# A fused attention, gating and channel-mix kernel on one core: another list of order for the opening and for the attention's pairs, and eleven pieces of the opening on another engine or queue

## The chip, the cores and the metric

The kernel runs as one program on one core of a Trainium2 chip. Its five engines are TensorE (PE), VectorE (DVE), ScalarE (ACT), GpSimd (POOL) and SyncE (SP, which only issues transfers here); each runs its own list of instructions in order and waits on semaphores for the others. The metric is the time of one execution on the device in microseconds (us). Three runs of the kernel before took 661.72, 662.39 and 663.0 us; the median is 662.39. The profile comes from one execution of its own.

## What is computed

Inputs are float32; batch 4, 8 heads, 576 positions, head size 64. Only the attention lies in the part that is changed:

```python
scores = scale * np.matmul(q, k.transpose(0, 1, 3, 2))
causal = np.triu(np.ones((S, S), dtype=bool), k=1)
cum = np.cumsum(np.maximum(s, 0.0), axis=-1)
bias = -(cum[:, :, :, None] - cum[:, :, None, :])
scores = np.where(causal, -1e9, scores + np.minimum(bias, 0.0))
scores = scores - np.max(scores, axis=-1, keepdims=True)
attn = np.exp(scores)
attn = attn / (np.sum(attn, axis=-1, keepdims=True) + 1e-09)
x = np.matmul(attn, v)
```

What follows is a gated layer (relu of x @ w_in, normalisation, a mixing over positions with w_spatial, w_out) and a channel mix (shifted x, w_k, a square, w_v, a sigmoid gate by w_r).

## The kernel before, in words

The 32 heads are worked in 16 pairs (two heads of one batch). A pair p passes through four stages that different engines share:

- T(p), function `st_T`: q and k, loaded as float32 into `RAW`, are split into a rounded high part and a low rest. `wh` and `xh` copy the high parts of q and k, `ud` and `vd` copy these to a second place, `ul` and `vl` subtract to get the rests. They are written into one large tile, `big`, which holds three pairs. In the opening each runs per head (a digit 0 or 1 behind the name).
- S(p), `st_S`: twelve score matmuls `s0` to `s11` (L459; 64 to 448 columns, six a head). VectorE takes the row maximum of each with the mask (L465, tile `jk`, accumulated in `mx`). `Ma` and `Mb` turn a head's maxima by a transpose on TensorE (L477), copy them on ACT (L479, tile `mt`) and send them as a row into `big` (L480).
- E(p), `st_E`: scores again with the maxima and the running sums as extra rows of the contraction (L497, two matmuls each, `e0` to `e9`, and `ez`, L530), the exponential on ACT (L517, L534), the causal mask on GpSimd (L521, L535).
- V(p), `st_V`: values (L555, L556, L559; `a0` to `a4` for one head, `b0` to `b4` for the other), copied out by ACT (L570, `fa`, `fb`). The sums of the exponentials go through memory (`n1`, `n2`, `n2b`), and `n30` on VectorE and `n31` on GpSimd multiply by their reciprocal (L592).

Beside these run small steps that decode weights from float64, part by part: `dL` loads (L125), `dF` is on ACT (L133, L134), `dD` on VectorE and GpSimd (L139 to L147), `dT` splits, `dS` stores (L182).

Before the first scores the running sums of s must be there: `lds` loads s, `sums` (L378, L379) sums them, `bases` (L103 by VectorE, L109 by GpSimd) takes the value at the start of each block of 128, `sums2` (L387, a copy, L389) splits the rest. `rx00` and `rx01` (L396) send the rows for pair 0 into `big`, `augd` (L403) keeps those of all pairs in memory. Constants `cw0` to `cw2` and `cx0` to `cx2` fill the rows of `big` that stay the same.

The order is written by hand in strings of these names. `START` has the opening: T, S and E of pair 0, T and S of pair 1, T of pair 2, and, with a plus, the whole of step 1 (E(1), V(0), S(2), T(3)). `ORDER` is the list for the steps 2 to 12: step p holds E(p), V(p-1), S(p+1) and T(p+2). `ORDER13` and `ORDER14` are for the steps 13 and 14. Each engine's own list follows from the strings, from `ENGINE` (V VectorE, S ACT, P GpSimd, by key; the letters A, B, C ahead of a key are the pairs 0, 1, 2 of the opening) and from `QUEUE` (A: issued by ACT; anything else: by SP). ACT issues a transfer in its own list, between its other instructions.

Of the kernel before, what the change touches and what calls it, by code (L numbers as in the profile page):

```python
# [26 lines left out]
def tile_kernel(  # L27
# [665 lines left out]
    START = """mask pads0 cx0 dD dT cw0 tiny ldk01 lds ldk00 cx1 dL ldq1 ldq01 pads2 sums 0xh0 ltv0 0xh1 1wh1 dF
               cx2 ldq00 0wh1 0vd1 bases sums2 0vd0 0ul1 0wh0 dL rx00 cw1 ldk1 rx01 0ul0 s0 ldq2 augd 1rows 1xh1 s4
               s10 s11 s9 s1 0vl0 s3 lv1 s2 cw2 1wh0 s5 0ud1 s6 s8 Ma pads1 0ud0 2wh1 dL s7 1xh0 2ul1 dF 1ul0 lv0
               1vd1 Mb e0 1vd0 0vl1 1s0 1s4 ldk2 1s6 dD 1vl0 dL e1 1s2 ez 2wh0 1ul1 e5 1s11 2rows 2xh1 dS 1s3 2vd1
               2ud1 1ud0 1s8 1s1 +lv 1s5 e3 2xh0 1s7 ldq3 1Ma 2vd0 1s9 +s6 1ud1 1s10 e4 e9 +s5 ones 2vl1 e6 e8 e7
               2ul0 dF +s4 +s9 1Mb e2 dT 2vl0 +ldk ldq4 1vl1 +e0 +zero +wh +s3 +a0 +s2 +s0 dL +a3 +ul ldk3 +e1 2ud0
               +xh +e3 +a1 +e5 +s1 +a2 dF +a4 +fa +ud +s10 +e4 +ez +s8 +e7 +rows +Ma +s7 +b0 +b3 +b2 +s11 +b1 dS
               +Mb +b4 +fb +e2 +n1 +e9 +e8 +e6 +ldq dD"""  # L700
# [744 lines left out]
```

## Time and profile before

| | before |
|---|---|
| runs (median of 3) | 662.39 us |
| the profiled execution: its time | 659.89 us |
| its span, first to last instruction | 658.1 us |
| TensorE busy | 628.7 us (96%) |
| VectorE busy | 519.8 us (79%) |
| ACT busy | 418.4 us (64%) |
| GpSimd busy | 337.3 us (51%) |
| granted TensorE clock, mean | 0.999 |

Busy shares are means over stages with different limits; a stretch has to be read by itself. Matmuls are pipelined and their ends are modelled, so a busy TensorE isn't TensorE at its peak. The time of the execution lies 1.8 us above its span, and 2.5 us below the median of the runs.

### The profile page before, as it was taken

The numbers are of one execution on the slowest core, as the hardware profiler recorded it, in microseconds if no ns is written. First come the engines' busy times: TensorE is split into PE (matmuls) and PEld (weight loads), VectorE is DVE, ScalarE is ACT, GpSimd is POOL, SyncE is SP. The second block draws the span as 40 slices with busy tenths as digits, with TensorE's granted clock in tenths as the row PEclk, the third lists the DMA queues.
The fourth block names the chain that finished last, engine by engine and source line by source line (L and its number), as shares of the span: only waits on it lengthen the run. The fifth ranks groups of instructions, "written<-read, shape, count | busy, mean of one in ns | idle before, by whom it ended". The sixth has DMA issues, their size and how long they took to land.

```text
span 658.1 us, 12257 instructions
## 1 busy us (share of the span) xinstructions
PE 628.7 (96%) x4036; PEld 551.9 (84%) x4036; DVE 519.8 (79%) x1168; ACT 418.4 (64%) x942; POOL 337.3 (51%) x464
## 2 busy tenths in 40 slices
PE   2899999999998999999999999999999999999997
PEld 1576666766666889999999999999999999999996
DVE  9879999999973799998878984888675866777773
ACT  5688888888874465575565572657675855554441
POOL 6357877759697434768646874531221123322220
PEclk9999999999999999999999999999999999999999
DMA  6446566565539727866454597743337973333301
GB/s 153 114 112 173 140 153 155 144 165 148 140 94 287 208 97 213 235 205 202 139 192 138 174 340 249 290 150 100 118 120 234 370 252 120 119 99 97 97 33 65
DMA packets 92303, 109.12 MB, mean 166 GB/s; under 512 B 32443, under 2 KB 73563, under 8 KB 90448
## 3 DMA queue, kind: packets, MB, share of 16 engines
q1 hardware_dynamic: 91146, 107.06, 53.7%
q10 hardware_dynamic: 1094, 1.28, 0.8%
q8 instruction: 32, 0.52, 0.3%
q14 instruction: 31, 0.25, 0.1%
HBM read 69.77 MB, written 37.52 MB: 163 GB/s over the span
## 4 chain that ended last, share of the span: by engine, by line
PE 71%; DVE 13%; DMA 7%; issue 3%; ACT 3%; POOL 1%; SPq 1%; DVEq 0%; POOLq 0%; ACTq 0%
PE mm L1009 26%; PE mm L757 24%; PE mm L825 7%; DVE big L121 4%; PE ps L497 4%; DVE jk L465 3%; PE pv L559 3%; PE s L459 3%; DMA rd<-r 2%; PE pv L556 1%; DMA rb<-rd 1%; DMA r<-pt 1%; ACT pt L570 1%; DMA brow<-in_moe_w_spatial_dram 1%; DVE g L139 1%
## 5 line engine op out<-in xcount | busy, mean ns | idle before, releaser
L757 PE MATMUL mm<-big 128*128 128x288 f32 (+1 forms) x600 | 102.6, 330 | 0.0
L757 PEld LDWEIGHTS mm<-big 128*128 128x128 f32 x600 | 91.5, 188 | 8.6 <-issue 0.4
L497 PE MATMUL ps<-big 128*128 128x288 f32 (+3 forms) x320 | 88.3, 369 | 1.7 <-ACT e L517 1.5
L147 POOL TENSOR_TENSOR f<-f,raw 128x256 int32<-128x256 int32 x64 | 52.3, 818 | 48.5 <-DVE f L145 19.9
L517 ACT ACTIVATE e<-ps 128x288 f32<-128x288 f32 (+3 forms) x160 | 62.5, 418 | 14.4 <-PE ps L497 12.4
L497 PEld LDWEIGHTS ps<-big 128*128 128x128 f32 x320 | 56.1, 199 | 17.5 <-issue 7.1
L465 DVE CUSTOM_DVE_ANT_0 jk<-s,mask 128x320 bf16<-128x320 f32 (+4 forms) x160 | 62.6, 423 | 9.8 <-PE s L459 7.9
L459 PE MATMUL s<-big 128*128 128x288 f32 (+4 forms) x192 | 54.8, 351 | 15.5 <-DMA big<-big 11.6
L559 PE MATMUL pv<-e,vp 128*65 128x448 f32 (+2 forms) x192 | 64.1, 434 | 0.0
L825 PE MATMUL mm<-xs,vb 128*128 128x288 f32 x256 | 56.3, 295 | 0.8 <-DVE vb L121 0.8
L521 POOL TENSOR_SCALAR_AFFINE_SELECT e<-e 128x128 f32<-128x128 f32 x128 | 46.8, 388 | 17.6 <-ACT e L517 15.3
L459 PEld LDWEIGHTS s<-big 128*128 128x128 f32 x192 | 35.7, 206 | 22.8 <-issue 13.5
L757 PE MATMUL mm<-wo,gh 128*128 128x512 f32 x216 | 52.4, 391 | 0.0
L757 PE MATMUL mm<-gh,wo 128*128 128x288 f32 x256 | 51.7, 294 | 0.0
L981 POOL TENSOR_TENSOR gh<-hl,gh 128x512 fp32r<-128x512 f32 x9 | 15.6, 1737 | 67.7 <-ACT gh L1215 67.7
L1009 PE MATMUL mm<-big,vb 128*128 128x256 f32 x384 | 48.4, 279 | 0.5 <-ACT vf L1158 0.5
L1009 PEld LDWEIGHTS mm<-big,vb 128*128 128x128 f32 x384 | 47.1, 188 | 1.3 <-ACT vf L1158 0.7
L121 DVE TENSOR_TENSOR big<-qk,big 64x1152 fp32r<-64x1152 f32 (+1 forms) x37 | 46.6, 1265 | 2.1 <-ACT big L106 0.9
L757 PEld LDWEIGHTS mm<-wo,gh 128*128 128x128 f32 x216 | 39.3, 188 | 7.5
L825 PEld LDWEIGHTS mm<-xs,vb 128*128 128x128 f32 x256 | 42.7, 188 | 1.2 <-DVE vb L121 1.2
L757 PEld LDWEIGHTS mm<-gh,wo 128*128 128x128 f32 x256 | 41.2, 188 | 0.2
L559 PEld LDWEIGHTS pv<-e,vp 128*65 128x65 f32 x192 | 25.1, 137 | 18.3 <-issue 14.1
(178 smaller groups left out, 1622.3 us busy)
## 6 DMA issues: line engine op xcount, KB each, us to landing
qk<-in_qk_dram SPq DMA_DIRECT2D x28, 288.0 KB
vf<-kd SPq DMA_DIRECT2D x6, 1024.0 KB
kd<-rt SPq DMA_DIRECT2D x32, 144.0 KB
rb<-rd SPq DMA_DIRECT2D x15, 288.0 KB
raw<-in_moe_w_in_dram SPq DMA_DIRECT2D x16, 256.0 KB
vp<-in_v_dram SPq DMA_DIRECT2D x16, 256.0 KB
raw<-in_moe_w_k_dram SPq DMA_DIRECT2D x16, 256.0 KB
raw<-in_moe_w_v_dram SPq DMA_DIRECT2D x16, 256.0 KB
```

Of the source, the lines that this page charges most:

```text
L121: (nc.gpsimd if eng == "P" else nc.vector).tensor_tensor(op=ALU.subtract, **kw)
L147: nc.gpsimd.tensor_tensor(out=f, in0=f, in1=low, op=ALU.add)
L459: nc.tensor.matmul(out=ps[:, 0:kn], lhsT=W[g][:, h, 128 * i:128 * i + 128], rhs=X[g][:, x0:x0 + kn], start=True, stop=True,)
L465: nc.vector.tensor_tensor_reduce(out=jk[r0:128, 0:kn], in0=ps[r0:128, 0:kn], in1=mask[r0:128, m0:m0 + kn], scale=1.0, scalar=(dst if mid e ...
L497: nc.tensor.matmul(out=ps[:, o:o + b - a], lhsT=st[g][:, key0(h, 128 * j):key0(h, 128 * j) + 128], rhs=mv[g][:, h, 64 + a:64 + b], start=( ...
L517: nc.scalar.activation(out=e[:, o:o + n], in_=ps[:, 0:n], func=ACTF.Exp, scale=scale)
L521: nc.gpsimd.affine_select(out=d, in_=d, pattern=[[1, w]], base=0, channel_multiplier=-1, compare_op=ALU.is_ge, fill=0.0,)
L559: nc.tensor.matmul(out=pv[0:VW, 1, 448 - w:448], lhsT=lt, rhs=e[:, OFF[j]:OFF[j] + w] if j < 4 else es[p][:, w * h:w * h + w], start=False ...
L757: nc.tensor.matmul(out=ps, lhsT=x, rhs=y, start=(m == 0), stop=(m == n - 1))
L825: nc.tensor.matmul(out=o, lhsT=x[:, sc, dd], rhs=y[:, sc, t], start=(sc == 0 and m == 0), stop=False)
L981: (nc.gpsimd if ENGINE[key] == "P" else nc.vector).tensor_tensor(**kw)
L1009: nc.tensor.matmul(out=ps, lhsT=x, rhs=y, start=(m == 0 and nm in ("P1", "P2", "P5")), stop=(m == last_m), skip_group_check=True)
```

## The change

Nothing that is computed changes. Two strings of order are rewritten, `ORDER` (steps 2 to 12) and `START`; `ORDER13`, `ORDER14` and all behind them stay. In `ENGINE` five keys of the opening move: two fills go to ACT (`cx0` from VectorE, `cx2` from GpSimd), `bases` goes from VectorE to GpSimd, pair 0's `xh` of the second head from ACT to GpSimd and its `ud` from VectorE to ACT. In `QUEUE` six transfers move: the loads of k for pair 0's second head, of q for pair 1 and of k for pair 3 from ACT to SP, and pair 0's q of the second head and its two rows of maxima from SP to ACT.

```diff
     ENGINE = dict(
...
-        cx0="V", cx2="P", bs="V", Axh1="S", Aud1="V",
+        cx0="S", cx2="S", bs="P", Axh1="P", Aud1="S",
...
     QUEUE = dict(
...
-        ldq1="A", Ma="P", Mb="P", ldq01="P", ldk01="A", ldk3="A",
+        ldq1="P", Ma="A", Mb="A", ldq01="A", ldk01="P", ldk3="P",
...
-    ORDER = """s4 s0 wh dT s6 e0 s3 e1 ul a0 vd e4 dL n2 s8 a3 lv xh e5 ltv zero s11 s5 rows a1 n2b e3 a2 a4 fa e2
-               dD e6 s2 dS ud s1 s7 b0 vl b3 Ma ldk s10 n31 e9 dF s9 e7 b1 b2 Mb b4 fb n1 n30 e8 ez ldq"""
+    ORDER = """s0 dT s4 wh s6 e0 s3 e1 e4 a0 ul dL vd n2 s8 a3 lv ltv xh s5 e5 zero s11 e3 a2 a1 a4 fa rows dD ud
+               e6 s2 n2b e2 s7 dS s1 vl b0 s10 b3 Ma s9 ldk dF n31 e9 e7 b1 b2 Mb b4 fb n1 ldq n30 e8 ez"""
...
-    START = """mask pads0 cx0 dD dT cw0 tiny ldk01 lds ldk00 cx1 dL ldq1 ldq01 pads2 sums 0xh0 ltv0 0xh1 1wh1 dF
...
+    START = """dF ldq01 cw0 lds ones cx0 cx2 pads1 sums 0wh1 pads0 ldk00 bases 0xh0 ldq1 sums2 mask 1wh1 ldk01 cx1
...
```

VectorE's list at the start, up to the first row maximum. `big<-small` are fills of constants, `e` holds s and its sums, `qk` the loaded q and k. Before:

```order
L103 CAST big<-small 64x1280 x2
L644 MEMSET x_72 128x16
L365 MEMSET small 32x1
L378 TENSOR_SCALAR e<-e 32x576
L379 SCALAR_TENSOR_TENSOR e<-small,e 32x576
L103 CAST big<-e 32x512
L103 CAST big<-e 32x64
L387 TENSOR_TENSOR e<-e,big 32x576
L103 CAST big<-e 32x576
L389 TENSOR_TENSOR big<-e,big 32x576
L103 CAST big<-big 64x576
L121 TENSOR_TENSOR big<-qk_150,big 64x576 x2
```

VectorE's list at the same place now:

```order
L103 CAST big<-small 64x1280
L365 MEMSET small 32x1
L378 TENSOR_SCALAR e<-e 32x576
L379 SCALAR_TENSOR_TENSOR e<-small,e 32x576
L387 TENSOR_TENSOR e<-e,big 32x576
L103 CAST big<-e 32x576
L389 TENSOR_TENSOR big<-e,big 32x576
L121 TENSOR_TENSOR big<-qk_150,big 64x576
L644 MEMSET x_72 128x16
L103 CAST big<-big 64x576
L121 TENSOR_TENSOR big<-qk_150,big 64x576
L465 ISA jk,mx_156<-s,mask 128x320
```

One fill and the two instructions of `bases` have left; a small memset has moved behind the first subtraction.

ACT's list ahead of pair 0's first exponential (L517), after the four transfers of the sums (L396, L403). `mt` are the turned maxima. Before:

```order
L106 CAST big<-qk_151 64x576
L106 CAST big<-small 64x1280
L106 CAST big<-qk_151 64x576
L479 CAST mt<-s 5x128
L106 CAST big<-big 64x576
L106 CAST big<-qk_150 64x576
L106 CAST big<-qk_151 64x576
L133 ACTIVATE g<-raw 128x256
L134 ACTIVATE raw<-raw 128x256
L479 CAST mt<-s 5x128
L517 ACTIVATE e<-ps 128x288
```

ACT's list now, the last twelve rows of that stretch (between the transfers and these lie six more casts of 64x576 and a fill of 64x1280):

```order
L106 CAST big<-qk_151 64x576
L479 CAST mt<-s 5x128
L480 DMA big<-mt 1x5x128
L106 CAST big<-big 64x576
L133 ACTIVATE g<-raw 128x256
L134 ACTIVATE raw<-raw 128x256
L479 CAST mt<-s 5x128
L480 DMA big<-mt 1x5x128
L106 CAST big<-big 64x576
L106 CAST big<-qk_150 64x576
L106 CAST big<-big 64x576
L517 ACTIVATE e<-ps 128x288 x2
```

Between the transfers of the sums and the first exponential stand eleven casts of 64x576 now, five before, and two transfers that SP had.

TensorE's list around the first transpose of a common step (`pv` are values, `ps` exponent scores, `s` scores). Before:

```order
L497 MATMUL ps<-big 128x448 x2
L497 MATMUL ps<-big 128x288 x2
L459 MATMUL s<-big 128x448
L459 MATMUL s<-big 128x288 x2
L555 MATMUL pv<-e,vp_149 65x128
L556 MATMUL pv<-e,vp_149 65x448
L559 MATMUL pv<-e,vp_149 65x192
L477 MATMUL s<-ident,mx_156 5x128
L459 MATMUL s<-big 128x192
L497 MATMUL ps<-big 128x192 x2
L459 MATMUL s<-big 128x320
L497 MATMUL ps<-big 128x448 x2
```

TensorE's list at the same place now:

```order
L497 MATMUL ps<-big 128x288 x2
L459 MATMUL s<-big 128x448
L497 MATMUL ps<-big 128x448 x2
L459 MATMUL s<-big 128x288 x2
L555 MATMUL pv<-e,vp_149 65x128
L556 MATMUL pv<-e,vp_149 65x448
L459 MATMUL s<-big 128x192
L559 MATMUL pv<-e,vp_149 65x192
L477 MATMUL s<-ident,mx_156 5x128
L459 MATMUL s<-big 128x320
L497 MATMUL ps<-big 128x192 x2
L497 MATMUL ps<-big 128x448 x2
```

A 192-column score stands ahead of the transpose; the two scores of 288 columns are `s1 s7` before and `s7 s1` now, and the transpose needs `s1`.

## Rows read from the trace of the kernel before

**Rows 1.** Busy time by stretch: length, then PE, PEld, DVE, ACT, POOL; clock, DMA share, GB/s

```profile
0.00:11.60 11.60, 0.00 (x0) 0.02 (x1) 10.22 (x15) 5.88 (x8) 8.57 (x22) 1.00 0.71 166
11.60:19.10 7.50, 5.38 (x14) 3.33 (x14) 6.93 (x26) 4.00 (x6) 1.75 (x3) 1.00 0.44 106
19.10:32.90 13.80, 12.38 (x38) 9.10 (x39) 12.23 (x40) 8.81 (x21) 6.46 (x17) 1.00 0.48 121
32.90:45.60 12.70, 12.25 (x63) 9.10 (x62) 8.37 (x26) 10.67 (x25) 5.34 (x15) 1.00 0.46 115
...
57.00:183.00 126.00, 121.91 (x663) 85.58 (x662) 116.55 (x344) 106.25 (x223) 97.76 (x169) 1.00 0.57 148
```

**Rows 2.** Timeline of the first 28 us: start, us, engine, line, operation, tiles

```profile
1.24 1.65 DVE L103 CAST big<-small 64x1280 fp32r<-64x1280 f32 x2 [0.34 <-POOL small L69]
...
2.84 1.05 DVE L378 TENSOR_SCALAR e<-e 32x576 f32<-32x576 f32 x1
...
3.67 0.63 SPq L332 DMA_DIRECT2D qk<-in_qk_dram  x1
...
5.31 0.52 DVE L103 CAST big<-e 32x512 fp32r<-32x512 f32 x2
5.86 0.75 DVE L387 TENSOR_TENSOR e<-e,big 32x576 f32<-32x576 f32 x1
...
7.23 3.06 POOL L109 TENSOR_SCALAR big<-small 64x1280 fp32r<-64x1280 f32 x2
7.49 1.68 DVE L389 TENSOR_TENSOR big<-e,big 32x576 fp32r<-32x576 f32 x1
...
9.20 1.40 DVE L103 CAST big<-big 64x576 fp32r<-64x576 f32 x1
9.20 1.56 ACTq L396 DMA_DIRECT2D big<-big  x1
9.28 0.67 ACT L106 CAST big<-qk 64x576 fp32r<-64x576 f32 x1
10.53 2.62 DVE L121 TENSOR_TENSOR big<-qk,big 64x576 fp32r<-64x576 f32 x2
10.69 1.85 POOL L121 TENSOR_TENSOR big<-qk,big 64x576 fp32r<-64x576 f32 x1 [0.40 <-DVE big L103]
...
11.62 0.95 PE L459 MATMUL s<-big 128*128 128x288 f32 x3 [11.62 <-DMA big<-big]
...
13.18 0.46 DVE L465 CUSTOM_DVE_ANT_0 jk<-s,mask 128x288 bf16<-128x288 f32 x1
```

**Rows 3.** Groups of instructions by form, 0 to 46 us: count, busy, mean ns, idle before

```profile
L465 DVE CUSTOM_DVE_ANT_0 jk<-s,mask 128x288 bf16<-128x288 f32 x7 | 3.2, 455 | 0.1
...
L106 ACT CAST big<-qk 64x576 fp32r<-64x576 f32 x10 | 6.6, 668 | 7.6 <-DMA qk<-in_qk_dram 4.6 <-issue 2.9
...
L109 POOL TENSOR_SCALAR big<-small 64x1280 fp32r<-64x1280 f32 x2 | 3.1, 1542 | 0.1
...
L109 POOL TENSOR_SCALAR big<-qk 64x576 fp32r<-64x576 f32 x2 | 1.6, 820 | 1.6 <-DMA qk<-in_qk_dram 1.5
```

**Rows 4.** Timeline: first exponential, pair 1's second transpose, the first common pair's first scores

```profile
20.72 0.40 ACT L517 ACTIVATE e<-ps 128x288 f32<-128x288 f32 x1
...
32.95 0.41 PE L477 MATMUL s<-ident,mx 128*5 128x128 f32 x1
...
45.35 0.54 PE L459 MATMUL s<-big 128*128 128x192 f32 x3
```

**Rows 5.** Waits in the first 50 us: who waited for whom, total us, times, longest

```profile
ACT mt L479 <- PE s L477: 2.1, 2, 1.3
```

**Rows 6.** Eleven pairs, 57 to 183 us: waits, and one group by form

```profile
DVE jk L465 <- PE s L459: 2.6, 6, 0.6
...
PE s L477 <- DVE mx L465: 1.7, 8, 0.5
...
L465 DVE CUSTOM_DVE_ANT_0 jk<-s,mask,mx 128x288 bf16<-128x288 f32 x22 | 10.5, 514 | 0.0
```

More of the change, by code (lines that the diff above doesn't have):

```diff
@@ L115, in tile_kernel @@
-    QUEUE = dict(lds="P", ltq0="A", ltk0="P", ldq1="A", ldk1="P", rx00="A", rx01="P", augd="A", Ma="P", Mb="P", n13="A", d13="P", b13="P", n14="P", d14="A", b14="P", n15="A", d15="A", b15="A", ldq00="P", ldq01="P", ldk00="P", ldk01="A", ldq2="P", ldk2="P", ldq3="P", ldk3="A", ldq4="P", ldk4="P")
+    ENGINE = dict(dM="S", c1="V", c2="P", c3="V", c4="P", ka0="S", ka1="P", ka2="P", ka3="S", kA11="P", kA12="P", kA22="V", kS1="V", kS2="P", kS3="V", kS4="V", k1="V", k2="V", k3="V", k4="V", vH="V", vS="P", vA="V", vT="V", v1="V", v2="V", v3="V", v4="V", rs0="V", rs1="P", gC11="V", gC12="V", gC22="V", qC110="V", qC111="S", qC120="S", qC121="V", qC210="S", qC211="S", qC220="V", qC221="S", n30="V", dH="P", dO="P", n31="P", xe0="P", xe1="V", xe2="P", xe3="P", xe4="P", gl0="V", gl1="V", gl2="V", gl3="V", cw0="V", cx0="S", cw1="P", cx1="S", cw2="S", cx2="S", bs="P", sc="V", N130="V", N131="V", N140="P", N141="V", N150="V", N151="V", wh="S", xh="P", ud="S", vd="S", ul="V", vl="V", Awh0="S", Axh0="S", Aud0="S", Avd0="V", Aul0="V", Avl0="P", Awh1="S", Axh1="P", Aud1="S", Avd1="S", Aul1="V", Avl1="V", Bwh0="S", Bxh0="S", Bud0="P", Bvd0="S", Bul0="V", Bvl0="V", Bwh1="P", Bxh1="S", Bud1="S", Bvd1="P", Bul1="V", Bvl1="V", Cwh0="P", Cxh0="S", Cud0="S", Cvd0="V", Cul0="V", Cvl0="V", Cwh1="S", Cxh1="S", Cud1="S", Cvd1="P", Cul1="V", Cvl1="V", ph0="S", pl0="V", ph1="S", pl1="V", ph2="S", pl2="V", ph3="S", pl3="P", ph4="S", pl4="V")
@@ L117, in queue @@
+    QUEUE = dict(lds="P", ltq0="A", ltk0="P", ldq1="P", ldk1="P", rx00="A", rx01="P", augd="A", Ma="A", Mb="A", n13="A", d13="P", b13="P", n14="P", d14="A", b14="P", n15="A", d15="A", b15="A", ldq00="P", ldq01="A", ldk00="P", ldk01="P", ldq2="P", ldk2="P", ldq3="P", ldk3="P", ldq4="P", ldk4="P")
     def queue(key):
@@ L691, in tile_kernel @@
         start.update({nm if nm in PARTS else "+" + nm: f for nm, f in st_.items()})
-    START = """mask pads0 cx0 dD dT cw0 tiny ldk01 lds ldk00 cx1 dL ldq1 ldq01 pads2 sums 0xh0 ltv0 0xh1 1wh1 dF
[L694 to L700, printed above, removed]
+    START = """dF ldq01 cw0 lds ones cx0 cx2 pads1 sums 0wh1 pads0 ldk00 bases 0xh0 ldq1 sums2 mask 1wh1 ldk01 cx1
+               0xh1 ldq00 0wh0 rx00 0ul0 augd tiny 0vd0 0ul1 dL 0ud0 ldk1 s3 1wh0 0vd1 rx01 0ud1 s4 0vl0 1xh0 s2 s0
+               ldq2 cw1 lv0 s9 s6 cw2 1ud1 s5 s11 1ul1 dL s10 s1 s8 pads2 1xh1 2wh0 s7 1rows Ma 1vd0 dL 1vd1 dF Mb
+               1ul0 0vl1 2ud0 1vl0 1s5 1s4 2rows dD 2wh1 1s11 ltv0 2ud1 1s0 e0 1s3 ldk2 ldq3 dT 1s2 e1 2xh0 dS 1s1
+               1s6 e5 1vl1 1Ma 1s9 1ud0 1s10 2xh1 ez lv1 +s4 e6 +s6 +lv 2vd1 1s8 e2 1s7 e7 e4 2vd0 e9 +s5 2ul0 dD
+               2ul1 1Mb ldk3 +s0 e8 dL e3 2vl0 +s1 +a0 dS dF +s3 +zero +e0 2vl1 +rows +e3 +wh +a1 +a2 ldq4 +ul +a3
+               +a4 +fa +s2 dD dL +s9 +s8 +ud +e5 +e9 +b0 +e6 +xh +b2 +Ma dF +b1 +e1 +ldq +b3 +b4 +ldk +s7 +s11 +fb
+               +n1 +e2 +e4 +s10 +ez +Mb +e8 +e7 dT"""
     for nm in START.split():
```

1 line of the change is left out of this document (removed).

## The prediction

> **What bounds the kernel now.** I read the busy time by stretch first [rows 1]. Two stretches are touched: the opening (start to 45.4 us, where the written-out list ends and the first pair under the common list begins) and the pairs 2 to 12. Until 11.6 us TensorE does nothing, and VectorE is busy 10.22 of these 11.60 us; from there to 32.9 us VectorE is busy 6.93 of 7.50 and 12.23 of 13.80 us, so it sets the pace. From 32.9 to 45.6 us TensorE has 12.25 of 12.70 us and VectorE only 8.37. In the pairs both are nearly full (121.91 and 116.55 of 126 us). The clock is granted in full throughout.
>
> Then the timeline of the start [rows 2]. The reader should follow one chain on VectorE: two fills of constants (1.24 to 2.89), the running sums of s (from L378 to 5.3), their bases (L103 on 32x512 and 32x64, to 5.83), L387, a cast, and L389, which ends at 9.17. Only then can the rows of the sums be sent (ACT's queue, L396, 9.20); the first score matmul starts when they have landed, 11.62. VectorE then has three more instructions (L103 at 9.20, two subtractions L121 until 13.15), so the first row maximum (jk) is at 13.18. VectorE, not the matmul, is last there.
>
> **The change, part by part: the start.** Five keys change engine and six transfers change queue; that the lists are rewritten is the larger part.
>
> (a) Before the sums VectorE now has one fill instead of two, 0.8 us less (1.65 for both [rows 2]). The sums also wait for s; that it has landed by 2.84 is all the trace shows. Gain 0 to 0.8; I take 0.2, since it was the first transfer of its queue and the row transfer took 2.4 us to land (9.20 to 11.62), which would put it near the old start.
>
> (b) The bases go to GpSimd. On VectorE they took 0.52 for both [rows 2]. On GpSimd a fill of 1280 columns takes 1.54, so 576 columns take 0.69 or more; a copy of 576 takes 0.82 [rows 3]. Loss 0.2 to 0.5; I take 0.3, the copy's row.
>
> (c) L389 took 1.68, while L387, a subtraction of the same shape, took 0.75 [rows 2]. GpSimd was then in its two fills (7.23, 3.06 for both). One of these goes to ACT, the other stands later. Gain 0 to 0.93; I take 0.6, as GpSimd has two casts of 0.82 near there.
>
> (d) The three instructions until the first jk took 4.0 us (9.17 to 13.18). Casts of 576 columns in all took 0.52 (L103 at 5.31) and a subtraction 0.75, so 2.0 at best, 4.0 at worst; I take 3.0, a gain of 1.0, because GpSimd still has a subtraction there (1.85 before [rows 2]).
>
> Sum: 0.2 - 0.3 + 0.6 + 1.0 = 1.5 us earlier, first jk at 11.7; from -0.5 to 3.6. TensorE can follow: sums sent at about 8.7, landed 2.4 later at 11.1, one score matmul, then jk.
>
> The Trainium skill (SBUF — State Buffer, Who interferes with whom) says that a VectorE instruction with two SBUF inputs and a GpSimd instruction that reads SBUF exclude each other for a whole instruction. By that rule, the trace agrees in kind: 1.68 beside GpSimd's fills, 0.75 without [rows 2]. It speaks against moving the bases and a cast to GpSimd; by it (d) would cost 4.7 instead of 3.0, which is the first rival below.
>
> The transfers. q for pair 0's second head goes ahead on ACT's queue, three loads of q and k go to SP; each costs its queue about 0.63 us of issue (SP at 3.67 [rows 2]). No queue that they leave or join was last before 9.2 us, so I put them at nothing. Up to and with q for the first head, 936 KB are now ahead instead of 1,320 (sizes from the order: 72, 144, 128, 256 and 288 KB). If that cover were gone, its cast would be late: it began at 9.28 before [rows 2], and VectorE now wants it at 8.7. The two transfers of pair 0's maxima hold ACT instead of SP: priced with ACT.
>
> **To the fourth transpose.** The transposes (L477) of row maxima, two a pair, mark progress: pair 1's second is at 32.95 [rows 4]. By the order, VectorE does before it one jk, two subtractions and two casts less than before: 0.46 [rows 3] + 2 x 0.75 + 2 x 0.52 = 3.0 us. As VectorE sets the pace there, I take all of it; 0 if TensorE holds it. It comes at 32.95 - 1.5 - 3.0 = 28.5.
>
> **From there to the first common pair.** That took 12.4 us (32.95 to 45.35 [rows 4]). Now VectorE has some 2.0 us more there (what was left out above, less one cast that went to ACT) and TensorE 0.3 more (one score matmul, two 320-column exponent pairs for one of 448). VectorE was idle 4.3 of 12.7 us [rows 1], so the cost is 0.3 to 2.0; I take 1.3, since TensorE, with 12.25 of 12.70, has little room.
>
> ACT has more before pair 0's first exponential, which was at 20.72 [rows 4]: 11 casts of 0.67 [rows 3] for 5 and two transfers of 0.63, 5.3 us more. It starts on them 0.5 earlier and had waited 2.1 for the transposes [rows 5], so the exponential comes up to 5.3 - 0.5 - 2.1 = 2.7 later, at 23.4. I cost this at nothing, because ACT then has done the casts that lay between exponentials before, and because TensorE waits for VectorE's maxima until 28.5. If that cover is gone it is the rival on the slower side.
>
> Opening: 1.5 + 3.0 - 1.3 = 3.2 us less.
>
> **The pairs (11 of them).** SP's and GpSimd's lists hardly change: one add (L147) moves ahead of one mask, and the wait for the broadcast stands at the same place on SP's queue. ACT does one copy earlier and two exponentials after it; TensorE has a 192-column exponent pair earlier. What counts is the first transpose: it needs the jk of head 0's last part, which now comes behind one of head 1's, 0.51 us [rows 6]. At worst 11 x 0.51 = 5.6 us. At best the list takes away all 2.6 us that jk waited for matmuls [rows 6]. TensorE waited for maxima at transposes only 1.7 us, in 8 of 22 cases [rows 6], and most of what it now waits at the first it has to spare at the second: I take 0.03 a pair, 0.3 us lost, nearest to that row.
>
> **Sum.** 3.2 - 0.3 = 2.9 us less than the profiled execution's 659.89, 657.0; the median of the runs, 662.39, stands 2.5 above it, and the forecast for that median is 662.39 - 2.9 = **659.5**.
>
> **Rivals.**
> 1. VectorE and GpSimd take turns: VectorE's three instructions of (d) each wait for a GpSimd one (0.82, 0.82 and 1.1, what of 1.85 lies beyond 0.75): 2.0 + 2.7 = 4.7 instead of 3.0. The gain is 2.9 - 1.7 = 1.2: 661.2, within 0.2%. For it: 1.68 and 1.85 in [rows 2]. Against: GpSimd's casts wait for loads and may fall elsewhere.
> 2. The hand-over gives it back: if the added VectorE work stretches the last part by all 2.0 and the pairs lose 0.1 each, the gain is 1.5 + 3.0 - 2.0 - 1.1 = 1.4: 661.0, on the border of no change. For it: both engines' shares in the pairs [rows 1].
> 3. Slower: ACT becomes the bound. Its casts put the first exponential 2.7 us later; that decides if TensorE comes to a matmul that waits for pair 0's exponentials before they are there, the transposes of pair 1 being early or not. Then the opening is 2.7 longer: 665.1. For it: ACT's list. Against: ACT was busy only 4.00 of 7.50 and 8.81 of 13.80 us [rows 1].
> 4. Better: the start at its best, 3.6, the last part at 0.3, the pairs as before: 3.6 + 3.0 - 0.3 = 6.3 less, 656.1.
>
> That the change does nothing is excluded, since the order on every engine differs until pair 12.
>
> **How the numbers follow.** Forecast 0.45, rival 1 0.14, rival 2 0.12, rival 3 0.14, rival 4 0.15. A measurement of this kernel tells 0.2%, 1.3 us, from no change. Rival 1, half of rival 2 and a little of the forecast fall within it (0.21); faster 0.65, slower 0.14. The range goes from 656.8, near rival 4, to 662.6, past rivals 1 and 2: it leaves out rival 3 and the edge of 4.
>
> **What would show it.** First jk near 11.7 and first matmul near 11.1; L389 near 1.1; the fourth transpose near 28.5; the first common pair's scores near 42.2 instead of 45.35; pairs of the same length within 0.1 us. A first exponential near 23.4 with no later stall means that ACT was covered. I am wrong if the fourth transpose is early and the first common pair is not, or if the pairs change by more than 1 us in all.

## The result, and the profile after

The change made the kernel faster: 8.75 us less in this comparison, three times the 2.9 us that were forecast, and outside the range (656.8 to 662.6). Where it was run again later (`after_again` below) it was 7.1 us less.

| | before | after |
|---|---|---|
| median of the runs of this comparison | 662.3 us | 653.55 us (652.5 to 656.43) |
| ratio, 95% interval | | 0.9874 (0.984 to 0.9909): 8.75 us less |
| the profiled execution: time, span | 659.89, 658.1 us | 656.43, 654.5 us |
| VectorE, ACT, GpSimd busy | 519.8, 418.4, 337.3 us | 512.3, 419.9, 345.5 us |

The two profiled executions differ by 3.46 us only, near the forecast's 2.9. But the profiled execution of before is faster than all its runs here, and the one of after is the slowest of its four. So the traces had to be taken again before they could be read against the runs.

The busy time by stretch in the first trace of the kernel after, same stretches and columns as [rows 1]:

```profile
0.00:11.60 11.60, 0.04 (x1) 0.07 (x1) 6.69 (x12) 7.05 (x8) 7.64 (x28) 1.00 0.58 141
11.60:19.10 7.50, 6.03 (x16) 3.85 (x16) 6.66 (x26) 6.14 (x10) 3.11 (x5) 1.00 0.70 180
19.10:32.90 13.80, 10.72 (x44) 9.10 (x44) 11.45 (x40) 9.59 (x24) 6.20 (x13) 1.00 0.41 101
32.90:45.60 12.70, 12.38 (x72) 9.32 (x71) 10.82 (x33) 11.79 (x25) 7.11 (x18) 1.00 0.64 152
57.00:183.00 126.00, 122.60 (x673) 86.58 (x673) 114.76 (x350) 106.15 (x226) 108.66 (x177) 1.00 0.56 147
```

Until 11.6 us VectorE (third engine column) is busy 6.69 instead of 10.22 us: it is no longer what TensorE waits for. The timeline of the start, and three marks further on, in the first trace of the kernel after (columns as in [rows 2]):

```profile
6.83 0.75 DVE L389 TENSOR_TENSOR big<-e,big 32x576 fp32r<-32x576 f32 x1
8.16 0.67 ACT L106 CAST big<-qk 64x576 fp32r<-64x576 f32 x1 [0.94 <-DMA qk<-in_qk_dram]
8.30 1.31 ACTq L396 DMA_DIRECT2D big<-big  x1
11.56 1.19 PE L459 MATMUL s<-big 128*128 128x320 f32 x3 [11.56 <-DMA big<-big]
12.32 0.49 DVE L465 CUSTOM_DVE_ANT_0 jk<-s,mask 128x320 bf16<-128x320 f32 x1 [1.65 <-PE s L459]
...
23.41 0.96 ACT L517 ACTIVATE e<-ps 128x288 f32<-128x288 f32 x2
...
30.85 0.27 PE L477 MATMUL s<-ident,mx 128*5 128x128 f32 x1
...
45.79 0.22 DVE L580 RECIPROCAL r<-r 128x9 f32<-128x9 f32 x1
```

L389 ends at 7.58 (9.17 before), yet ACT sends the rows of the sums only at 8.30: in its list a cast stands ahead that waits 0.94 us for a load of q. The rows took 3.26 us to land, reckoned to the start of the first matmul, which waits for them. The last row is a mark that I use below: the reciprocal (L580), of which each common step has one; in step 2 it is at 49.09 us before (the expectations call it recip).

### The profile page after: what moved, and what is told of

The parts are those of the page before. It is cut to its first block, busy times and chain, and to the rows that moved or that the text cites. A ratio compares the mean times of both kernels' runs of the same rounds, so it can differ in the third digit from the quotient of the medians.

```text
span 654.5 us, 12259 instructions
## 1 busy us (share of the span) xinstructions
PE 624.8 (95%) x4036; PEld 550.5 (84%) x4036; DVE 512.3 (78%) x1164; ACT 419.9 (64%) x944; POOL 345.5 (53%) x466
## 4 chain that ended last, share of the span: by engine, by line
PE 84%; DMA 6%; DVE 4%; ACT 3%; issue 2%; SPq 1%; POOL 0%; ACTq 0%; DVEq 0%; POOLq 0%
PE mm L757 27%; PE mm L1009 27%; PE mm L825 8%; PE pv L559 7%; PE ps L497 6%; PE s L459 3%; PE pv L556 3%; DMA e<-in_moe_w_spatial_dram 1%; DMA r<-pt 1%; DMA qk<-in_qk_dram 1%; PE pv L555 1%; DVE jk L465 1%; PE s L477 1%; DMA big<-mt 1%; PE mm L827 1%
## 5 line engine op out<-in xcount | busy, mean ns | idle before, releaser
L147 POOL TENSOR_TENSOR f<-f,raw 128x256 int32<-128x256 int32 x64 | 54.1, 845 | 59.6 <-DVE f L145 27.9
L497 PE MATMUL ps<-big 128*128 128x288 f32 (+3 forms) x320 | 75.9, 340 | 2.3 <-DMA big<-mt 1.2
L459 PE MATMUL s<-big 128*128 128x288 f32 (+4 forms) x192 | 62.8, 378 | 16.1 <-DMA big<-big 11.6
L517 ACT ACTIVATE e<-ps 128x288 f32<-128x288 f32 (+3 forms) x160 | 60.4, 420 | 8.1 <-PE ps L497 6.5
L459 PEld LDWEIGHTS s<-big 128*128 128x128 f32 x192 | 36.5, 205 | 28.5 <-issue 13.0
L521 POOL TENSOR_SCALAR_AFFINE_SELECT e<-e 128x128 f32<-128x128 f32 x128 | 54.0, 444 | 11.4 <-ACT e L517 9.2
L497 PEld LDWEIGHTS ps<-big 128*128 128x128 f32 x320 | 52.0, 195 | 8.5 <-ACT e L517 2.9
L121 DVE TENSOR_TENSOR big<-qk,big 64x1152 fp32r<-64x1152 f32 (+1 forms) x37 | 46.0, 1246 | 3.2 <-ACT big L106 1.9
```

Of the source, the lines that this page charges most:

```text
L121: (nc.gpsimd if eng == "P" else nc.vector).tensor_tensor(op=ALU.subtract, **kw)
L147: nc.gpsimd.tensor_tensor(out=f, in0=f, in1=low, op=ALU.add)
L459: nc.tensor.matmul(out=ps[:, 0:kn], lhsT=W[g][:, h, 128 * i:128 * i + 128], rhs=X[g][:, x0:x0 + kn], start=True, stop=True,)
L497: nc.tensor.matmul(out=ps[:, o:o + b - a], lhsT=st[g][:, key0(h, 128 * j):key0(h, 128 * j) + 128], rhs=mv[g][:, h, 64 + a:64 + b], start=( ...
L517: nc.scalar.activation(out=e[:, o:o + n], in_=ps[:, 0:n], func=ACTF.Exp, scale=scale)
L521: nc.gpsimd.affine_select(out=d, in_=d, pattern=[[1, w]], base=0, channel_multiplier=-1, compare_op=ALU.is_ge, fill=0.0,)
```

## Experiments

All runs below are timed against the kernel before on the same chip. Read from each kernel's one trace, where not said otherwise: the first row maximum (jk), pair 1's second transpose (L477), the reciprocal of step 2, and how long the eleven steps from there took. From the reciprocal of step 14 to the end all traces took 472.1 to 475.6 us, without order between the kernels; what the change does lies ahead of that, but a single trace carries these 3.5 us of chance too.

| kernel | ratio to before, 95% interval | first jk | 2nd L477 of pair 1 | step 2 | eleven steps |
|---|---|---|---|---|---|
| before, first and second trace | 1.0 (0.9986 to 1.0013) | 13.18, 13.29 | 32.95, 33.05 | 49.09, 48.88 | 124.8, 122.9 |
| after, first and second trace | 0.9893 (0.9877 to 0.9909) | 12.32, 10.95 | 30.85, 28.56 | 45.79, 43.38 | 123.2, 121.9 |
| opening_only | 0.9918 (0.9901 to 0.9934) | 11.07 | 29.18 | 44.00 | 125.5 |
| pairs_only | 0.9971 (0.9955 to 0.9986) | 13.29 | 33.05 | 48.72 | 124.5 |
| keys_back | 0.9922 (0.9896 to 0.9948) | 12.98 | 32.33 | 47.28 | 124.8 |
| keys_only | 1.0077 (1.0059 to 1.0096) | 17.06 | 37.96 | 52.95 | 125.8 |
| engines_back | 0.9939 (0.9918 to 0.9959) | 11.90 | 31.32 | 46.10 | 123.6 |
| queues_back | 0.994 (0.9921 to 0.996) | 11.80 | 31.62 | 46.92 | 121.9 |
| fills_late | 0.9996 (0.998 to 1.0011) | 12.91 | 32.67 | 47.79 | 122.6 |
| fill_early | 0.9927 (0.9903 to 0.9952) | 11.59 | 29.58 | 44.35 | 123.6 |
| rx00_first | 0.9898 (0.987 to 0.9926) | 11.96 | 29.65 | 44.40 | 124.5 |
| new_then_old | 0.9937 (0.9912 to 0.9961) | 11.34 | 28.64 | 45.71 | 123.6 |
| no_xh | 0.9843 (0.9813 to 0.9873) | 11.10 | 28.29 | 43.11 | 120.3 |
| dd_late | 1.0042 (1.0026 to 1.0059) | 11.06 | 29.07 | 43.89 | 133.0 |
| xh_after_dd | 0.9885 (0.9865 to 0.9905) | 11.12 | 29.06 | 43.89 | 123.6 |
| s1_first | 0.9898 (0.9869 to 0.9927) | 11.01 | 28.31 | 43.17 | 123.7 |

### Where the gain lies: both kernels again, and the two halves of the change

`before_again` and `after_again` have no edit.

`before_again`, expected:

> The kernel before, unchanged, for a second trace and for the size of chance. Theory A (the few us beyond the forecast are the difference between one execution and the next, and lie behind the pairs, where both traces wait for the transfers r<-pt and the weights of the mixing, 187 to 226 us): ratio 1.000 within 0.002, the third recip of the pairs and all up to 186 us within 0.3 us of the first trace, and what this execution's span has over or under 658.1 appears between 186 and 226 us. Theory B (each execution of before is slower through the pairs than the one profiled): the pairs' twelve steps take over 137.5 us instead of 136.7.

`after_again`, expected:

> The changed kernel, unchanged, for a second trace. Its first profiled execution was its slowest of four (656.4 against 652.5 to 654.2). Theory A: time near 653.5, ratio near 0.987; the twelve steps take 135.1 us within 0.3 as in the first trace, and a shorter span than 654.5 comes from the stretch 181 to 219 us, where the lead over before fell from 5.0 to 3.2 us. Theory B: the twelve steps are shorter by 1 us or more than in the first trace.

`opening_only` is the kernel before with the new `START`, `ENGINE` and `QUEUE`; `pairs_only` has the new `ORDER` alone. The core of the second:

```diff
-    ORDER = """s4 s0 wh dT s6 e0 ...
+    ORDER = """s0 dT s4 wh s6 e0 ...
```

`opening_only`, expected:

> Kernel before with the new START and the eleven moved keys, the old ORDER. If the opening's lead of 3.3 us (recip of step 2 at 45.79 against 49.09) is kept to the end: 659.0, ratio 0.995. If the larger part of the 8.75 us is the opening's: 656 or less. If the lead is lost behind the pairs, since the transfers there start by their own queue: 661 to 662.4, ratio 0.998 to 1.000.

`pairs_only`, expected:

> Kernel before with the new ORDER alone. By the forecast: +0.3 us, ratio 1.000. By the two traces (0.14 us a pair less, eleven or twelve of them): 660.7, ratio 0.9975, twelve steps in 135.1 us instead of 136.7. If the timed gain that the traces don't show is the pairs': 657 or less, ratio 0.992 or less.

The two traces of before have the same span, 658.1 us, by cancelling: the second is 1.9 us shorter in the eleven steps and 2.2 us longer behind step 14. So neither theory on before holds. The second trace of after, the fastest of its five executions as the first was the slowest of its four, has a span 5.0 us shorter. Its twelve steps are shorter by 1.28 us, which meets theory B's mark of 1 us; another 1.3 us lie behind step 14. The largest part lies where neither theory had looked: step 2 is reached 2.41 us earlier, at 43.38. Its start:

```profile
6.85 0.75 DVE L389 TENSOR_TENSOR big<-e,big 32x576 fp32r<-32x576 f32 x1
7.44 0.67 ACT L106 CAST big<-qk 64x576 fp32r<-64x576 f32 x1 [0.22 <-DMA qk<-in_qk_dram]
7.76 1.54 ACTq L396 DMA_DIRECT2D big<-big  x1
8.14 0.75 DVE L121 TENSOR_TENSOR big<-qk,big 64x576 fp32r<-64x576 f32 x1 [0.54 <-ACT big L106]
10.19 2.74 PE L459 MATMUL s<-big 128*128 128x320 f32 x6 [10.19 <-DMA big<-big]
10.95 0.49 DVE L465 CUSTOM_DVE_ANT_0 jk<-s,mask 128x320 bf16<-128x320 f32 x1 [0.54 <-PE s L459]
```

The load of q came 0.72 us earlier, the rows were sent at 7.76 and took 2.43 us to land. In the seven other traces whose list is as changed up to the rows (opening_only, new_then_old, no_xh, dd_late, xh_after_dd, s1_first, and fill_early, which has one fill more on GpSimd there) the rows were sent at 7.81 to 8.12 and the first matmul was at 10.24 to 10.58. So the first profiled execution had an unusually late start. I call after_again and these seven, without fill_early, the usual traces. Those of them that have no edit ahead of step 2 (all but new_then_old) reach it at 43.11 to 44.00, so that the opening is worth 4.9 to 6.0 us, not 3.3. The timed run agrees: opening_only is 0.82% (5.4 us) faster than before. The new `ORDER` alone gives 0.29%, 1.9 us (0.9 to 3.0).

### The start: what sets the first row maximum

`fills_late` moves two fills in the `START` of before, `fill_early` one in that of after, and `rx00_first` swaps two names in that of after:

```diff
# fills_late
-               cx2 ldq00 0wh1 ... 0wh0 dL rx00 cw1 ldk1 ...
+               ldq00 0wh1 ... 0wh0 dL rx00 ldk1 ...
-               s10 s11 s9 s1 0vl0 s3 ...
+               s10 s11 s9 s1 0vl0 cx2 cw1 s3 ...
# fill_early
-               0xh1 ldq00 0wh0 ... ldq2 cw1 lv0 ...
+               0xh1 cw1 ldq00 0wh0 ... ldq2 lv0 ...
# rx00_first
-               0xh1 ldq00 0wh0 rx00 0ul0 ...
+               0xh1 ldq00 rx00 0wh0 0ul0 ...
```

`fills_late`, expected:

> The kernel before with GpSimd's two fills (cx2, cw1; 3.06 us for both at 7.2 to 7.7 us) moved in START to behind its subtraction, into the 7 us in which it waits for the first exponential. Nothing else changes. Theory P: VectorE's L389 falls from 1.10 or 1.68 to 0.75, L103 from 1.40 to about 0.5, the two L121 from 2.6 or 3.7 to 1.5 to 2.0; the first jk comes at 11.8 or when the rows have landed, 1.4 us earlier than 13.2 to 13.3, and 1 to 1.5 us come off the whole: 659.5 to 660. Theory L (the load of q and k and the rows' transfer behind ACT's cast hold the start): first jk 12.8 or later, no change that can be told.

`fill_early`, expected:

> The changed kernel with one fill of constants on GpSimd (cw1, 64x1280, 1.25 us at 11.8 to 12.0 us in the traces of the change) put back to just behind pair 0's two casts of k, so that it runs beside VectorE's cast and two subtractions at 8.1 to 10.4 us. Theory P (VectorE and GpSimd hold each other up there; that the fills are gone from this place is what the start gained): these three take 3.0 to 4.0 us together as before the change instead of 2.3, the first jk comes at 11.9 to 12.6 instead of 10.95 to 11.07, and the whole is 0.8 to 1.5 us slower than the change: about 655. Theory R (the landing of the rows of sums sets the first jk): the first jk stays within 0.2 us and the time at 653.5 to 654.3.

`rx00_first`, expected:

> The changed kernel with the rows of the sums (rx00) issued by ACT ahead of the cast of q (0wh0) that waits for a load. The rows then go as soon as L389 is done. Theory Q: sent at 7.6 to 7.7 in place of 7.76 to 8.30, first matmul at 10.1, first jk 10.9 at the latest if VectorE's subtraction isn't later: 0.1 to 0.7 us faster than the change, 653 to 654. Rival: the cast now stands behind the issue (1.5 us on ACT's queue), so VectorE's three instructions come 0.3 to 1.5 us later and set the first jk at 11.3 or later: same or 0.5 us slower.

The start of fills_late:

```profile
8.08 0.67 ACT L106 CAST big<-qk 64x576 fp32r<-64x576 f32 x1 [2.16 <-DMA qk<-in_qk_dram]
8.26 0.46 DVE L103 CAST big<-big 64x576 fp32r<-64x576 f32 x1
8.78 0.67 ACT L106 CAST big<-big 64x576 fp32r<-64x576 f32 x1
8.78 0.75 DVE L121 TENSOR_TENSOR big<-qk,big 64x576 fp32r<-64x576 f32 x1
9.40 1.31 ACTq L396 DMA_DIRECT2D big<-big  x1
10.17 1.24 DVE L121 TENSOR_TENSOR big<-qk,big 64x576 fp32r<-64x576 f32 x1 [0.63 <-ACT big L106]
12.18 0.95 PE L459 MATMUL s<-big 128*128 128x288 f32 x3 [12.18 <-DMA big<-big]
12.91 0.46 DVE L465 CUSTOM_DVE_ANT_0 jk<-s,mask 128x288 bf16<-128x288 f32 x1 [1.51 <-PE s L459]
```

VectorE's three instructions fell to 0.46, 0.75 and 1.24 us, as theory P wanted (L389 kept its 1.10, beside a cast of k on GpSimd), but the first jk came only 0.3 to 0.4 us earlier, as theory L wanted: L389 is done at 8.23, the rows leave at 9.40 behind ACT's casts of q, which wait for loads, and land at 12.18. The second trace of before has the same wait:

```profile
7.13 1.10 DVE L389 TENSOR_TENSOR big<-e,big 32x576 fp32r<-32x576 f32 x1
...
8.17 0.67 ACT L106 CAST big<-qk 64x576 fp32r<-64x576 f32 x1 [2.32 <-DMA qk<-in_qk_dram]
...
9.65 0.67 ACT L106 CAST big<-qk 64x576 fp32r<-64x576 f32 x1
9.66 1.31 ACTq L396 DMA_DIRECT2D big<-big  x1
```

So the kernel before had two chains of nearly equal length: VectorE's three instructions end at 13.26, and if the first scores take the 0.73 us until jk that they took in fills_late, the rows' chain ends at 12.6. Taking VectorE out of GpSimd's way shortens one, and the other holds the end. The trace of fills_late, the fastest of its twelve executions, has step 2 1.1 to 1.3 us earlier than before; its timed runs show no gain (0.9996).

fill_early shows the reverse: with the second chain short, a fill beside VectorE's last subtraction (1.79 instead of 0.74 us) puts the first jk at 11.59, 0.6 us later than in after_again, and step 2 1.0 us later; the first jk falls short of theory P's 11.9, and the run is 0.34% (2.2 us) slower than after's, somewhat more than it said. rx00_first went by its rival: the rows left at 7.83, when L389 was done, but the cast behind them began at 9.42, and VectorE set the first jk, at 11.96; the time can't be told from after's.

Which of the keys shortens the second chain? The edits put back the five engine keys, the six queue keys, or both into after; `keys_only` puts all eleven into before:

```diff
# in ENGINE: engines_back, keys_back (keys_only the other way round)
-... cx0="S", cx2="S", bs="P", Axh1="P", Aud1="S" ...
+... cx0="V", cx2="P", bs="V", Axh1="S", Aud1="V" ...
# in QUEUE: queues_back, keys_back (keys_only the other way round)
-... ldq1="P", Ma="A", Mb="A", ldq01="A", ldk01="P", ldk3="P" ...
+... ldq1="A", Ma="P", Mb="P", ldq01="P", ldk01="A", ldk3="A" ...
```

`engines_back`, expected:

> The changed kernel with its five engine keys as before (one fill, the bases and one cast more on VectorE, a fill more on GpSimd, pair 0's last xh on ACT); lists and queues as changed. Theory Q (the loads and the rows' place in ACT's list set the start): q of the first head lands as in the change, rows sent at 8.0 to 8.6, first jk at 11.0 to 11.7, at most 1 us slower than the change: 654 to 655. Theory V (VectorE sets it): rows sent at 8.3 or later by L389, first jk 12.3 or later, 655.5 or more.

`queues_back`, expected:

> The changed kernel with its six queue keys as before; lists and engines as changed. SP then loads q of pair 0 ahead of s, and ACT the 288 KB of q for pair 1. Theory Q: s late by about 1 us (L378 at 3.8 as with both sets of keys back), ACT's cast ahead of the rows late (9.7), first jk at 12.5 to 13.0, 2 us or more slower than the change: 656 or more. Theory V: first jk within 0.5 us of the change's 11.0, 653.5 to 654.5.

`keys_back`, expected:

> The changed kernel with the eleven keys of engines and queues as before, both new lists kept. VectorE has one fill (0.75), the two bases (0.52) and one cast (0.44) more ahead of the fourth transpose, GpSimd one fill more, and SP issues the rows of maxima. If the keys carry the start: first jk at 12.0 or later instead of 11.0, and 1.5 us or more slower than the change, 655 to 657. If the lists carry it: within 0.7 us of the change, 653 to 655.

`keys_only`, expected:

> The kernel before with the eleven keys alone, its lists kept. If the keys are worth something only with the new list: within 0.3% of before, 659.3 to 662. If they carry the start by themselves: first jk at 11.5 or earlier and 1.5 us or more off the kernel before, below 659.5. If the old list with these keys brings a load late (s or q behind a larger one): first jk over 13.3, slower than before.

By time, engines_back went as theory V said and queues_back as theory Q: both halves of the keys count, 0.46% and 0.47% (3 us) each. Both first jk lie between the forecasts of the two (11.90 and 11.80), so the start alone can't be where the 3 us are lost. With the queues back, q is loaded ahead of s and the sums start 1.2 us later; with the keys alone, s comes later still, and the bases stand behind a cast on GpSimd that waits for a load. The rows of queues_back, then of keys_only:

```profile
3.86 0.45 DVE L378 TENSOR_SCALAR e<-e 32x576 f32<-32x576 f32 x1 [1.83 <-DMA e<-in_s_dram]
8.87 1.32 ACTq L396 DMA_DIRECT2D big<-big  x1
```

```profile
4.54 0.46 DVE L378 TENSOR_SCALAR e<-e 32x576 f32<-32x576 f32 x1 [2.48 <-DMA e<-in_s_dram]
10.11 0.81 POOL L109 TENSOR_SCALAR big<-e 32x512 fp32r<-32x512 f32 x2
10.95 1.78 DVE L387 TENSOR_TENSOR e<-e,big 32x576 f32<-32x576 f32 x1 [4.57 <-POOL big L109]
14.12 1.31 ACTq L396 DMA_DIRECT2D big<-big  x1
```

The 0.85 us that queues_back loses at the first jk are gone again at pair 1's first transpose: 24.60 us, where the usual traces have 24.13 to 24.84. Its second comes 7.0 us behind the first, in after_again 3.8. What I had overlooked lies between them. Pair 0's two rows of maxima are sent by SP again, at 19.09 and 20.71; the loads of k for pair 2 and of q for pair 3 stand behind them in SP's list and leave at 22.70, in after_again at 18.11. ACT's cast of that k waits 2.58 us for the load, and TensorE's next scores wait 1.66 us for ACT. Rows of queues_back:

```profile
26.77 0.67 ACT L106 CAST big<-qk 64x576 fp32r<-64x576 f32 x1 [2.58 <-DMA qk<-in_qk_dram]
...
27.54 0.33 PE L459 MATMUL s<-big 128*128 128x192 f32 x1 [1.66 <-ACT big L106]
```

So most of the queues' 3 us is read from this one wait; the two keys `Ma` and `Mb` were not tried by themselves.

The lists alone give 0.78% (keys_back), the keys alone cost 0.77%, and together they give 1.07%: no part can be priced without the other.

### The last part of the opening

`new_then_old` keeps the new `START` up to `1Mb` and puts the rest in the old order:

```diff
-... 1Mb ldk3 +s0 e8 dL e3 2vl0 +s1 +a0 dS dF +s3 +zero +e0 2vl1 +rows +e3 +wh ...
+... 1Mb dL e3 2vl1 e8 dF +s9 dT 2vl0 +ldk ldq4 +e0 +zero +wh +s3 +a0 +s2 +s0 ...
```

> The changed kernel whose START follows the new list through pair 1's second transpose (1Mb) and puts what is left in the order of the old list. From that transpose to the recip of step 2 the trace of before has 15.8 to 16.1 us, of the change 14.8 to 14.9. If the sequence of the last part is what makes it shorter: 15.8 or more again, 1 us slower than the change, about 655. If the last part is shorter since the front has left it other work: 14.9 again and the change's time, 653.5 to 654.3.

From pair 1's second transpose to step 2 it took 17.07 us (28.64 to 45.71), against 14.82 in after_again and 15.83 to 16.14 in the two traces of before. The sequence of this part is what makes it shorter; with the old one behind the new front it is even longer than before, and the run is 0.44% (2.9 us) slower than after. The eleven other traces with the whole new list took 14.75 to 15.30 us here.

### The pairs

`no_xh` leaves GpSimd's cast `xh` out for the pairs 4 to 14; the other three move names in the new `ORDER`:

```diff
# no_xh
+                if a == "xh" and 4 <= p <= 14:
+                    items[a + e] = lambda: None
# dd_late
-... fa rows dD ud e6 s2 n2b e2 s7 dS s1 vl b0 ...
+... fa rows ud e6 s2 n2b e2 s7 s1 dD dS vl b0 ...
# xh_after_dd
-... a3 lv ltv xh s5 e5 ... fa rows dD ud ...
+... a3 lv ltv s5 e5 ... fa rows dD xh ud ...
# s1_first
-... n2b e2 s7 dS s1 vl ...
+... n2b e2 s1 dS s7 vl ...
```

`no_xh`, expected:

> The changed kernel without GpSimd's cast of k's high part (xh, 64x1152, 1.15 us alone) for the pairs 4 to 14; left out of the computation, to see what it costs the pairs. Theory C (the pairs' length is set by where GpSimd's instructions meet VectorE's; L139, L141 and L145 take 0.3, 0.3 and 0.4 us alone, and one of them 1.2 to 1.3 when it meets this cast, in about two pairs of three): none of the three above 0.8, pairs of 10.8 to 11.0 us instead of 11.1 to 11.2 on average, 2 to 4 us less than the change: 650 to 652. Theory E (TensorE, busy 97% of the pairs, sets their length): pairs within 0.1 us of the change's, time 653 to 654.5.

`dd_late`, expected:

> The changed kernel with the weights' step dD (VectorE L139, L141, L145, then GpSimd L147) put behind the scores s2 s7 s1 in ORDER, so that it stands behind the two row maxima and does not meet GpSimd's cast xh. Theory C: the three take 0.3, 0.3 and 0.4 us in nearly all pairs, the first transpose gets its maxima about 1 us earlier, pairs 0.1 to 0.4 us shorter: 649 to 653. Rival: VectorE then waits for the scores where dD stood (up to 1 us a pair) and dD meets another GpSimd instruction (L147 of its own, or a mask): same time or up to 5 us slower.

`xh_after_dd`, expected:

> The changed kernel with GpSimd's cast xh moved in ORDER from ahead of s5 to behind dD, so that it runs beside the row maxima that follow (jk kept its 0.62 us beside xh in the trace of the change) and not beside L139, L141 and L145. Theory C: the sum of the three falls from about 1.6 us a pair to 1.1 to 1.3, pairs to about 10.9 as without the cast (10.91 on average over eleven), 650 to 652. Rival: xh now meets the subtraction L121 behind the maxima (1.35 alone), which gives back what is won: 653 to 655.

`s1_first`, expected:

> The changed kernel with s1 again ahead of s7 in ORDER: the forecast's own mechanism, taken away. Forecast: the first transpose gets its maxima up to 0.51 us earlier, of which 0.03 a pair counts: 0.3 us faster than the change, not to be told from it, 653 to 654.3. If the wait was costly: up to 5.6 us faster, 648. If the new sequence of the two is part of the gain in the pairs (one less wait of the second head): 1 to 2 us slower, 655.

Without the cast the eleven steps took 120.3 us instead of 121.9 to 123.2, and the run 0.5% less than after's own: that cast has a price in the pairs. In this trace L139, L141 and L145 each took 0.74 us at most (up to 1.29 in after), and VectorE's L592 (`n30`), which GpSimd's (`n31`) delays where that begins first, took 0.75 in all eleven steps. Theory C, that the price is such meetings of GpSimd's instructions with VectorE's, fits; but with the cast its data are left out too, so that what waits for them starts earlier, and that was not told apart. One meeting with the cast and one of the two L592, in opening_only:

```profile
67.93 1.15 POOL L109 TENSOR_SCALAR big<-qk 64x1152 fp32r<-64x1152 f32 x1
67.95 1.28 DVE L139 TENSOR_SCALAR g<-g 128x256 f32<-128x256 f32 x1
...
73.30 1.40 POOL L592 TENSOR_TENSOR x<-pt,rb 64x576 f32<-64x576 f32 x1 [2.23 <-DMA rb<-rd]
73.76 1.55 DVE L592 TENSOR_TENSOR x<-pt,rb 64x576 f32<-64x576 f32 x1
```

L139 takes 0.29 us where it meets nothing. The step with these two took 12.04 us; the next, with L139 at 0.59 and VectorE's L592 at 0.75, took 10.78. Over the 99 steps of the nine traces that have the new `ORDER` unedited, the time of L139, L141, L145, VectorE's L592 and L121 accounts for 86% of the differences in length (a least-squares fit of mine, so an association and no proof).

The two attempts to keep them apart failed by their rivals. In xh_after_dd L139, L141 and L145 took 1.1 us a step in all, but in two steps the cast met the subtraction behind the maxima, and those took 12.27 and 12.26 us:

```profile
59.02 1.15 POOL L109 TENSOR_SCALAR big<-qk 64x1152 fp32r<-64x1152 f32 x1
59.16 2.21 DVE L121 TENSOR_TENSOR big<-qk,big 64x1152 fp32r<-64x1152 f32 x1
```

In dd_late the meetings of L139 are gone, and from the fourth on the steps take 12.19 or 12.20 us, all alike: VectorE now waits for scores, and in every one GpSimd's L592 begins first, so that VectorE's takes 1.97 instead of 0.75 us. Which of the two sets the length was not tried. The waits of dd_late from 43.8 to 177 us:

```profile
DVE jk L465 <- PE s L459: 17.9, 13, 1.6
...
PE s L477 <- DVE mx L465: 7.8, 11, 0.7
```

s1_first can't be told from after (0.9898 against 0.9893, each within 0.0029 or less): the order of these two scores is worth nothing that can be measured here. None of these can be told to beat after but no_xh, which doesn't do all the work.

## Why the forecast was too small

**Which terms failed.** The forecast was 1.5 (start) + 3.0 (to the fourth transpose) - 1.3 (to the first common pair) - 0.3 (pairs) = 2.9 us less. Measured, the first two are 2.3 and 2.2 us less; the last two are 1.1 and 1.9 us less, where I had put a loss. The first two were off by 0.8 us each way, which cancels by luck. The miss is in the other two, 2.4 and 2.2 us, both with the wrong sign. Beside these, one step that I put at nothing was not nothing: the transfers. Rival 4 (656.1) came nearest, but it too kept a loss of 0.3 in the last part and no gain in the pairs.

**What bounds the start.** "Only then can the rows of the sums be sent" and "VectorE, not the matmul, is last there" saw one of two chains. In before_again L389 was done at 8.23, 0.9 us earlier than in the first trace, and the rows left no earlier, at 9.66, behind ACT's casts. VectorE was last in both traces, as said, but by 0.7 to 0.8 us only. The first jk was forecast at 11.7; it came at 10.95 to 11.34 in the usual traces, 1.8 to 2.3 us earlier than before instead of 1.5, with bounds that held it (their upper end adds up to 3.5, not 3.6).

**The transfers.** "No queue that they leave or join was last before 9.2 us, so I put them at nothing." By queues_back they are worth 3 us. The queues set when s and q land, and the rows stand behind casts that wait for q; that is 0.85 us at the first jk. The larger part comes later and was not looked for: two rows of maxima on SP's queue hold back loads that stand behind them. That these two "hold ACT instead of SP" saw what they cost the engine that they join, not what they free on the queue that they leave.

**Terms (a) to (d).** (a) gained 0.1 to 0.2 at the start of L378, but L378 itself took 0.45 instead of 1.05 us, so that the scan behind it (L379) began 0.75 to 0.77 earlier, near the best end of (a), 0.8; in the traces of before L378 ran beside GpSimd's memset of the mask, which now comes later. (b) cost 0.4: VectorE waited 0.95 us for the bases, which had taken it 0.52. L389 fell to 0.75, the best end of (c). In after_again the three instructions of (d) took 0.75, 0.90 and 0.74 us, 2.4 in all; but from the end of L389 to the first jk it was 3.35 and not 3.0, since VectorE waited 0.54 us for ACT's cast and 0.54 for the first scores. The first rival (turns with GpSimd, 4.7) fell: GpSimd's fills no longer stand there. fill_early shows that its mechanism is right, where one does.

**To the fourth transpose.** Forecast 28.5. The usual traces have 28.3 to 29.2; the sum of two terms was right, by the luck named above: a larger share for the start and a smaller one here, 2.2 us (19.77 to 17.61) instead of 3.0. VectorE did 2.4 us less there (17.66 to 15.27 busy), and set the pace, as said. The first trace after has 30.85: 1.4 us of that is its late start. TensorE now waits for ACT's copies of the maxima (1.7 and 2.5 us in the two traces) and for their transfer (1.2 and 0.7), where before only its weight loads waited (0.6 and 0.4); that this took the rest of the 3.0 is read from the waits and wasn't tried.

**From there to the first common pair.** Forecast +1.3, bounds 0.3 to 2.0; measured -0.9 to -1.3 to the reciprocal of step 2 (-0.7 to -1.1 to the first common scores, the mark named in the forecast), outside the bounds. This is the largest miss: 2.4 us. These scores were forecast near 42.2, and the first trace has them at 42.26; that is luck, as its late start hides the gain here. In after_again they are at 39.85. VectorE's added work was right (8.32 to 9.98 us busy, 1.7 for my 2.0). Wrong was that it must cost something, "since TensorE, with 12.25 of 12.70, has little room". TensorE's busy time is no measure of its work there: the same form took longer before. The forms of 448 columns before (32.95 to 45.35 us), and in after_again (28.56 to 40.00 us):

```profile
L497 PE MATMUL ps<-big 128*128 128x448 f32 x6 | 2.3, 473 | 0.0
...
L459 PE MATMUL s<-big 128*128 128x448 f32 x2 | 1.1, 562 | 0.0
```

```profile
L497 PE MATMUL ps<-big 128*128 128x448 f32 x4 | 1.2, 384 | 0.0
...
L459 PE MATMUL s<-big 128*128 128x448 f32 x2 | 0.8, 406 | 0.0
```

With the other sequence 66 matmuls fit into the 11.29 us up to the first common scores where 61 took 12.40 (by the lists it is three more; some records are missing). Two of the six matmuls in the first group took 0.72 and 0.58 us, the others 0.36 to 0.45. What held these up is not shown.

**ACT.** The first exponential came at 23.41 and 23.08 (forecast 23.4), and the opening still ended early. Rival 3 fell.

**The pairs.** Forecast +0.3 us; the timed run of the new `ORDER` alone says -1.9 (-3.0 to -0.9), which is past the 1 us that I had named as the mark of an error. The mechanism of that term, the wait behind `s7`, can't be told from nothing (s1_first); the transposes' waits, 1.7 us in [rows 6], are 0.8 and 0.5 in the two traces of after and 1.8 in that of pairs_only, which decides nothing. What I left out is that a step's length goes with which instructions of GpSimd and VectorE meet, up to 1.2 us a step. Which move in `ORDER` gains the 1.9 us, and by what, stays open: the eleven steps vary by some 3 us between traces with the same `ORDER` (121.9 to 124.8 with the new one, 122.6 to 125.8 with the old; the means, 123.5 and 124.3, differ by less), and the shares of L139 over 0.4 us (58 of 99 steps with the new, 27 of 55 with the old) and of VectorE's L592 behind GpSimd's (25 of 99, 13 of 55) are about the same.

**From the profile to the median.** "The median of the runs stands 2.5 above it" was carried over as a constant. It isn't one: the profiled execution of after lay at the other end of its runs. Over 23 more executions before took 659.38 to 662.73 us.

The sum as measured (the first three from the traces of before and after_again, the pairs from the timed run): start -2.3, middle -2.2, last part -1.1, pairs -1.9: 7.5 us less, against 7.1 us (1.07%) in the larger comparison and 8.75 in the first.

## What to carry to other kernels

Follow every instruction that stands ahead of a critical transfer in the list of the engine that issues it, not only the producer of its data: a cast that waits for a load held the rows back about as long as the arithmetic did. Ask of a transfer that changes queue not only what it costs there, but also what stood behind it where it was. A busy share near full is no proof that an engine has no room; compare the mean duration of one form between stretches. And where the gain sought is under 1%, take a second trace of the kernel before you build on the time of one.
